# Half-pair transposes in two PSUM banks, joined decay sums and paired mixer tiles in a chunked recurrence with a token mixer

## The chip, the cores and the metric

The kernel runs on one core of a Trainium2 chip. Five engines work side by side and meet at semaphores: TensorE (PE in the profile; PEld is its weight load), VectorE (DVE), ScalarE (ACT), GpSimd (POOL) and SyncE (SP), which only issues DMA here. PE writes only into PSUM, eight banks of 2 KB on each of 128 partitions; DVE and ACT read PSUM, POOL does not. The metric is the time of one execution on the device in microseconds (us).

## The reference

Two stages, in float32 outside and bfloat16 in the matmuls. The first is a linear recurrence per batch and head (4 batches, 8 heads, 768 tokens, 40 features):

```python
for t in range(S):
    y[:, :, t] = np.einsum('bhd,bhde->bhe', rt, state)
    Sa = np.einsum('bhde,bhe->bhd', state, at)
    state_decay = state * wt[:, :, None, :] - np.einsum('bhd,bhe->bhde', Sa, bt)
    state = state_decay + np.einsum('bhd,bhe->bhde', vt, kt)
```

The second takes the heads side by side as x (4 x 768 x 320) and mixes tokens, then channels:

```python
theta = x @ w_theta
zr, zi = x * np.cos(theta), x * np.sin(theta)
yr = np.einsum('ts,bsd->btd', w_tok_r, zr)
yi = np.einsum('ts,bsd->btd', w_tok_i, zi)
u = x + yr + yi
return (u + np.maximum(u @ w_ch, 0.0)).astype(np.float32)
```

## The kernel before

**Tiles.** A tile is 128 tokens of one batch, all 8 heads: 6 tiles a batch, 24 in all. The recurrence is done a tile at a time, with the state carried between the tiles of a batch.

**Attention of one tile.** `prep` (L439) takes the logarithm of w, sums it down the tokens by a matmul with a triangle (L461), and gets the decay products by Exp (L469). A second set, without the token's own decay, is needed for a and for the output: for the first 7 tiles (`EXCLUSIVE`) by another triangle matmul (L476) and Exp (L479), later by DVE adding the logarithm back (L482) and an Exp (L487). k and b are multiplied by the one set and a by the other (L429), and all are cast to bfloat16. Then kb, a and v are transposed on PE, 128 x 128 blocks against an identity (L391), into one bank a tensor, and copied out by ACT or DVE (L394, L397). For the first 8 tiles (`RUNS`) v, and for all tiles r, come by DMA in runs of eight tokens and are transposed by `turn_runs` (L538); `turn_back` (L557) makes the token-major v of the first 8. Eleven groups, listed in `CROSSBAR`, are transposed by DMA on SP's queue instead (L698).

`attention_scores` and `readout` form four 128 x 128 score blocks per head (psi, phi, lamv, lamu) with matmuls of 64 rows, two heads at once on the two halves of the array into two banks (L569). Each result is masked by DVE while it leaves PSUM (L578), or scaled by ACT (L580) and then masked by POOL's select (L582). `recurrence` solves for the tile (x0 L610 and L616, nx, nu L629) and makes the new state gt (L652). From the fifth tile on (`FROM_POOL`) DVE adds the old state (L663) and POOL multiplies by the decay (L667); before that PE adds it by an identity matmul (L647). `readout` forms y (L793, L800, L802), and L809 scales it to x.

**Mixer.** `theta` transposes two tiles of x as five blocks (L711) and multiplies them by w_theta: two matmuls a tile over 128 rows (L763) and, for the 64 rows that are left of each, one of half height, the two side by side (L773). Results are copied tile by tile (L828). When a batch's tiles are through, `sines` takes Sin in two groups of three tiles (L850), which needs another table of ACT, and POOL multiplies (L865), zr and zi apart. `mix_row` sums 12 matmuls for each output tile (L881), `channels` multiplies by w_ch in the same way as theta, and each output tile is stored by its own DMA (L920). The rows of one batch run between the attention of the next.

**Order.** The order of all work is written out: `add` collects the operations, and `Plan.order` emits them by the list `ORDER`. `PICK` names those that run on their second engine, `HOMES` gives each PSUM result its bank, from four single banks and two pairs, and `WARM` puts 49 idle matmuls before some early operations. Each engine runs its own operations in this order.

Of the kernel before, what the change touches and what calls it, by code (L numbers as in the profile page):

```python
# [17 lines left out]
BANKS = 8  # L18
DOUBLE = 4
FROM_POOL = 4  # L20
EXCLUSIVE = 7
RUNS = 8
LAST = (22, 23)
CROSSBAR = (("tkb", 23), ("ta", 23), ("tv", 22), ("tv", 23), ("xt", 18), ("xt", 20), ("ut", 12), ("ut", 14),
            ("ut", 16), ("nut", 21), ("nut", 22))
ORDER = [
# [118 lines left out]
WARM = {21: 25, 30: 4, 33: 1, 28: 8, 41: 11}  # L145


class Op:
# [908 lines left out]
```

## Time and profile before

| | |
|---|---|
| two runs | 199.07 and 200.09 us, median 199.58 |
| profiled execution, first to last instruction | 197.8 us |
| granted TensorE clock | 1.00 |
| HBM read, written | 29.54 MB, 3.93 MB |
| input load, issue to landing (raw_w, raw_r) | 4.1, 4.4 us |

Most lines of the profile give an engine, an operation, output<-inputs by the program's names, shapes and a count, then busy time in us and mean length in ns, and behind a second bar the idle time of the engine just before, with what ended it. `128*128` in front of the shapes is the part of the array that is used; `64*128` is half its rows. In the answers by stage, each stretch has the busy time and the count of instructions of PE, PEld, DVE, ACT and POOL, then the granted clock, the share of the DMA engines and GB/s.

### The profile page before, as it was taken

The page shows a single profiled execution, that of the slowest core. Times are in us where ns is not written, and L with a number is a line of the kernel's source. Part 1 is how long each engine was busy: PE and PEld are TensorE (multiplying, and loading weights), DVE is VectorE, ACT ScalarE, POOL GpSimd, SP SyncE. Part 2 cuts the span into 40 slices and gives each one's busy share as a digit, 9 for nine tenths or more (in the row PEclk, how much of TensorE's full clock was granted, in tenths as well). Part 3 has the DMA queues.
Part 4 walks back from the last instruction along what each step waited for, and adds up shares of the span by engine and source line. Part 5 has one row for each costly group of instructions (what it writes and reads, how often), then busy time and mean ns, then how long its engine had stood idle before and what let it go on. Part 6 is the DMA issues. An engine that isn't in the chain of part 4 may idle for free.

```text
span 197.8 us, 8019 instructions
## 1 busy us (share of the span) xinstructions
PE 187.6 (95%) x3288; PEld 150.3 (76%) x3288; DVE 164.3 (83%) x261; ACT 151.7 (77%) x337; POOL 145.1 (73%) x210
## 2 busy tenths in 40 slices
PE   7888999999989999999999999999999999999992
PEld 6776787777768788878878888888887878767661
DVE  5269899999989999888887988999999988675453
ACT  3584979799889988979988598888998986575111
POOL 8267544679879999699799939769699697558100
PEclk9999999999999999999999999999999999999999
DMA  6999879989999999999998899988998274863055
GB/s 119 210 212 163 154 161 196 182 166 197 233 174 173 207 171 185 190 185 223 153 210 168 153 187 170 188 148 169 182 155 163 43 177 102 87 194 104 0 191 174
DMA packets 134644, 32.75 MB, mean 166 GB/s; under 512 B 124816, under 2 KB 134608, under 8 KB 134608
## 3 DMA queue, kind: packets, MB, share of 16 engines
q1 hardware_dynamic: 131680, 29.19, 75.1%
q0 software_dynamic: 2784, 2.97, 9.6%
q8 instruction: 25, 0.41, 0.9%
q10 hardware_dynamic: 144, 0.08, 0.1%
q14 instruction: 11, 0.09, 0.1%
HBM read 29.54 MB, written 3.93 MB: 169 GB/s over the span
## 4 chain that ended last, share of the span: by engine, by line
PE 68%; DMA 9%; ACT 8%; SPq 6%; DVE 3%; issue 3%; POOL 1%; ACTq 0%; DVEq 0%; POOLq 0%
PE ps_s L881 17%; PE ps_s L391 10%; PE ps_d L569 9%; PE ps_s L763 5%; SPq L409 4%; DMA raw_w<-in_w_dram 3%; DMA raw_kb<-in_k_dram 3%; PE ps_s L711 3%; PE ps_s L652 2%; PE ps_s L629 2%; SPq L421 2%; DMA raw_r<-in_r_dram 2%; PE ps_s L538 2%; PE ps_s L773 2%; ACT cs L850 2%
## 5 line engine op out<-in xcount | busy, mean ns | idle before, releaser
L429 POOL TENSOR_TENSOR kb<-raw_kb,ex 128x320 bf16<-128x320 f32 x46 | 36.8, 811 | 9.7 <-DMA raw_kb<-in_k_dram 3.3
L881 PE MATMUL ps_s<-zr,wtok_r 128*128 128x320 bf16 x132 | 37.6, 299 | 0.0
L881 PE MATMUL ps_s<-zi,wtok_i 128*128 128x320 bf16 x132 | 37.5, 299 | 0.0
L578 DVE TENSOR_TENSOR lamu<-ps_d,mask_p 128x1024 bf16<-128x1024 f32 x22 | 26.8, 1219 | 1.7 <-PE ps_d L569 1.6
L578 DVE TENSOR_TENSOR psi<-ps_d,mask_p 128x1024 bf16<-128x1024 f32 x22 | 26.8, 1218 | 1.6 <-PE ps_d L569 1.4
L578 DVE TENSOR_TENSOR lamv<-ps_d,mask_p 128x1024 bf16<-128x1024 f32 x17 | 20.7, 1218 | 2.6 <-PE ps_d L569 1.8
L429 POOL TENSOR_TENSOR ah<-raw_a,we 128x320 bf16<-128x320 f32 x22 | 19.0, 866 | 3.6 <-DMA raw_a<-in_a_dram 1.6
L578 DVE TENSOR_TENSOR phi<-ps_d,mask_n 128x1024 bf16<-128x1024 f32 x17 | 20.7, 1218 | 0.9 <-PE ps_d L569 0.8
L865 POOL TENSOR_TENSOR zi<-cs,xp 128x320 bf16<-128x320 f32 x21 | 16.9, 816 | 3.3 <-ACT cs L850 3.3
L881 PEld LDWEIGHTS <-wtok_r 128*128 128x128 bf16 x144 | 14.0, 97 | 4.5
L569 PE MATMUL ps_d<-aT,kbT 64*128 64x128 bf16 x384 | 17.1, 217 | 0.2
L881 PEld LDWEIGHTS <-wtok_i 128*128 128x128 bf16 x144 | 14.1, 98 | 3.5
L391 PE MATMUL ps_s<-wide,kb 128*128 128x128 bf16 x184 | 15.0, 223 | 1.0 <-POOL kb L429 0.7
L865 POOL TENSOR_TENSOR zr<-cs,xp 128x320 bf16<-128x320 f32 x19 | 15.3, 810 | 0.7 <-ACT cs L850 0.7
L667 POOL TENSOR_TENSOR gt<-sum,ex 128x320 bf16<-128x320 f32 x13 | 9.5, 733 | 8.0 <-DVE sum L663 4.8
L800 PE MATMUL ps_s<-kb,lamv 128*128 128x40 bf16 x192 | 15.0, 180 | 0.0
L802 PE MATMUL ps_s<-kb,lamu 128*128 128x40 bf16 x192 | 14.9, 179 | 0.0
L569 PEld LDWEIGHTS <-kbT 64*128 64x128 bf16 x384 | 11.8, 94 | 3.1 <-ACT kbT L394 1.0
L800 PEld LDWEIGHTS <-lamv 128*128 128x128 bf16 x192 | 13.2, 96 | 0.6
L887 DVE TENSOR_TENSOR up<-ps_s,xp 128x320 bf16<-128x320 f32 x22 | 10.7, 488 | 3.5 <-PE ps_s L881 3.1
L435 POOL CAST r<-raw_r 128x640 bf16<-128x640 f32 x12 | 8.6, 720 | 6.5 <-DMA raw_r<-in_r_dram 6.5
L445 ACT ACTIVATE lw<-raw_w 128x320 bf16<-128x320 f32 x24 | 11.4, 475 | 2.6 <-DMA raw_w<-in_w_dram 2.6
(176 smaller groups left out, 606.7 us busy)
## 6 DMA issues: line engine op xcount, KB each, us to landing
raw_w<-in_w_dram SPq DMA_DIRECT2D x24, 160.0 KB, 4.1
raw_v<-in_v_dram SPq DMA_DIRECT2D x24, 160.0 KB, 3.9
raw_a<-in_a_dram SPq DMA_DIRECT2D x24, 160.0 KB, 4.2
raw_kb<-in_k_dram SPq DMA_DIRECT2D x24, 160.0 KB, 3.7
raw_kb<-in_b_dram SPq DMA_DIRECT2D x24, 160.0 KB, 4.0
raw_r<-in_r_dram SPq DMA_DIRECT2D x24, 160.0 KB, 4.4
out_dram<-oo SPq DMA_DIRECT2D x9, 160.0 KB, 2.0
wrow_i<-in_moe_w_tok_i_dram POOLq DMA_DIRECT2D x6, 192.0 KB, 5.3
```

The source lines that it names most:

```text
L391: nc.tensor.transpose(out=dst[:, c:c + 128], in_=pair(src, g), identity=ident)
L429: pool = ("POOL", lambda: nc.gpsimd.tensor_tensor(out=dst, in0=in0, in1=in1, op=ALU.mult))
L445: add("ACT", "ln", i, lambda: nc.scalar.activation(out=paired(lw)[:, :, :, 0:D], in_=paired(raw_w[s4]), func=AF.Ln), 473, [("raw_w", s4)], ...
L569: nc.tensor.matmul(t[:, q, g, :], lhsT=lhs[g][rows(q)], rhs=rhs[g][rows(q)], start=True, stop=True)
L578: add("DVE", kindm, i, lambda: nc.vector.tensor_tensor(out=flat, in0=whole(), in1=mask.to_broadcast([128, 2 * G, 128]), op=ALU.mult), 1217 ...
L667: add("POOL", "wgt", i, lambda: nc.gpsimd.tensor_tensor(out=new_state, in0=sum_t, in1=wm.to_broadcast([128, 8, D]), op=ALU.mult), 830, [(" ...
L763: nc.tensor.matmul(ps(pk)[:, 0:DM], lhsT=lhs[:, 3 * c + kt, :], rhs=wt[:, 3 * c + kt, :], start=kt == 0, stop=kt == 2, skip_group_check=n ...
L800: nc.tensor.matmul(o, lhsT=lamv[:, p, g, :], rhs=kb[:, 0, h, 0:D], start=first, stop=False, skip_group_check=True)
L802: nc.tensor.matmul(o, lhsT=lamu[:, p, g, :], rhs=kb[:, 1, h, 0:D], start=False, stop=True, skip_group_check=True)
L865: pool = ("POOL", lambda: nc.gpsimd.tensor_tensor(out=dst, in0=in0, in1=in1, op=ALU.mult))
L881: nc.tensor.matmul(acc(), lhsT=wtok[nm][j][:, s], rhs=zs[c][:, s], start=n == 0 and c == 0, stop=n == NT - 1 and c == 1)
L887: add("DVE", "uadd", q, lambda: nc.vector.tensor_tensor(out=u, in0=acc(), in1=x, op=ALU.add), 488, [pk, x_key(q)], [u_key(q)], at="row")
```

## The change

- **Transposes.** `half_turns` transposes a 128-row block as two halves of 64 rows, one on each half of the array, each into its own bank of a pair. k, b and a of a tile go as one group of 12 blocks with one copy (`kbaT`), r and v of two tiles as one group (`turned`); after the eighth tile v has a group of its own for two tiles. Small groups (nu, x, u, `turn_back`) go either way, by `PICK`. DMA transposes are gone.
- **Decay.** The second decay sum is always a matmul with the strict triangle, into the bank beside the first, and one Exp reads both (`decays`). The DVE step L482 and the second Exp are gone. From the third tile on, k and b are one product of twice the width.
- **State.** The old state is always added by the identity matmul in `gt_mm`, and DVE alone makes the new state.
- **Mixer.** theta and channels run for two tiles as six matmuls over 128 rows into two banks, with zero rows in the weights in place of the half-height matmuls. One copy or one output step serves both tiles, one DMA stores both, and zr and zi are one product. Sin takes two groups of three tiles, and for the last batch four, one and one.
- **Order.** `ORDER`, `PICK`, `HOMES` and `WARM` are new. Any operation may use any bank, 96 idle matmuls are placed, and which engine copies, masks and multiplies is chosen anew for every operation.

The core of the diff:

```diff
-FROM_POOL = 4
-EXCLUSIVE = 7
+SPLIT = 2
...
+    def half_turns(key, srcs, first=0):
+        if plan.home[key][1] == 1:
+            for n, src in enumerate(srcs):
+                nc.tensor.transpose(out=block(bf(ps(key)), first + n), in_=src, identity=ident)
+            return
+        for n, src in enumerate(srcs):
+            for c in range(2):
+                to = bf(ps(key)[:, c])[:, (first + n) * 64:(first + n) * 64 + 64]
+                nc.tensor.transpose(out=to, in_=src[rows(c)], identity=ident[rows(c), rows(c)])
...
+            nc.tensor.matmul(sums(1)[:, :, 0:D], lhsT=mask_p[:, 0, :], rhs=lw[:, :, 0:D],
+                             start=True, stop=not total_of(i), skip_group_check=True)
+            if total_of(i):
+                nc.tensor.matmul(sums(1)[:, :, D], lhsT=mask_p[:, 0, :], rhs=lw[:, :, 63],
+                                 start=False, stop=True, skip_group_check=True)
...
+                nc.scalar.activation(out=ex.rearrange("p c h x -> p c (h x)"),
+                                     in_=ps(pk)[:, :, 0:DM + 8], func=AF.Exp)
...
+            product("kb", i, kb[:, :, :, 0:D], raw_kb[i % NK],
+                    ex[:, 0:1, :, 0:D].to_broadcast([128, 2, H, D]),
...
+        add("PE", "tkba", i, lambda: half_turns(
+            key, [pair(s, g) for s in (kb[:, 0], kb[:, 1], ah) for g in range(G)]),
...
-                add("POOL", "wgt", i, lambda: nc.gpsimd.tensor_tensor(
-                    out=new_state, in0=sum_t, in1=wm.to_broadcast([128, 8, D]), op=ALU.mult), 830,
...
-        def both():
-            for c in range(2):
-                nc.tensor.matmul(ps(("ps", kind, q + c))[:, 0:DM], lhsT=lhs[rows(c), 2, :],
-                                 rhs=wt[rows(c), 2, :], start=False, stop=True,
-                                 skip_group_check=True)
+        def both():
+            for c in range(2):
+                for kt in range(3):
+                    nc.tensor.matmul(ps(key)[:, c, 0:DM], lhsT=block(lhs, 2 * c + kt),
+                                     rhs=wt[:, 3 * c + kt, :], start=kt == 0, stop=kt == 2)
...
+            product("z", q, z[:, :, j], cs_t[:, :, j],
+                    x.rearrange("p (o d) -> p o d", o=1).to_broadcast([128, 2, DM]),
...
+WARM = {62: ((0, 42),), 114: ((1, 17),), 40: ((2, 20),), 28: ((4, 17),)}
```

More of the change, by code (lines that the diff above doesn't have):

```diff
@@ new lines, in gt_mm @@
+        def gt_mm():
+            t = ps(gk)
+            if not first:
+                nc.tensor.matmul(t[:, 0:DM], lhsT=ident,
+                                 rhs=gt_old.rearrange("p g c d -> p (g c) d")[:, :, 0:D],
+                                 start=True, stop=False, skip_group_check=True)
+            for g in range(G):
+                for j, (lt, rt) in enumerate(((kb[:, 0], vb), (kb[:, 1], nu))):
+                    nc.tensor.matmul(t[:, g * 80:g * 80 + 80], lhsT=pair(lt, g),
+                                     rhs=rt[:, 2 * g:2 * g + 2, 0:D],
+                                     start=first and j == 0, stop=j == 1, skip_group_check=True)
@@ L887, in mix_row, with chunk @@
+        x, u, z = x_of(q), u_of(q), z_t[bi % 2]
+        for s in range(NT):
+            def chunk(s=s):
+                for c in range(2):
+                    nc.tensor.matmul(ps(pk)[:, 0:DM], lhsT=wtok[j][:, c, s], rhs=z[:, c, s],
+                                     start=s == 0 and c == 0, stop=s == NT - 1 and c == 1)
+            add("PE", "row", q, chunk,
+                [("z", 0, bi % 2, s), ("z", 1, bi % 2, s), ("wtok", j)], [pk],
+                new=(pk, 1) if s == 0 else None)
         add("DVE", "uadd", q, lambda: nc.vector.tensor_tensor(
-            out=u, in0=acc(), in1=x, op=ALU.add), 488,
@@ new lines, in channels @@
+        ends = q == N - 1
+        halves = [slice(0, DM // 2), slice(DM // 2, DM)] if ends else [slice(0, DM)]
+        mixed("ch", q, uT_t[n], wch, [("wch", c) for c in range(6)], ("uT", n), halves)
+        bi, j = divmod(q, NCH)
+        place = (q + 1) // 2 % NO
+        oo = oo_t[place]
+        if not alone(q):
+            ck = ("ps", "ch", q)
+            add("DVE", "oo2", q, lambda: nc.vector.scalar_tensor_tensor(
+                out=oo.rearrange("p (c d) -> p c d", c=2), in0=ps(ck)[:, :, 0:DM], scalar=0.0,
+                in1=src.rearrange("p (c d) -> p c d", c=2), op0=ALU.max, op1=ALU.add),
+                [ck] + [u_key(t) for t in group], [("oo", place)])
+            store(q, out_p[bi, j // 2], oo.rearrange("p (c d) -> p c d", c=2), ("oo", place))
+            return
@@ new lines, in channels @@
+        for part, at in enumerate(halves):
+            ck = ("ps", "ch", q + part)
+            key = ("oo", place) if part == 0 else ("last", 1)
+            add("DVE", "oo1" if not ends else "ooh", q + part, lambda ck=ck, at=at:
+                nc.vector.scalar_tensor_tensor(
+                    out=oo[:, at], in0=ps(ck)[:, 0:at.stop - at.start], scalar=0.0,
+                    in1=u_of(q)[:, at], op0=ALU.max, op1=ALU.add),
+                [ck, u_key(q)] + ([("oo", place)] if part else []), [key])
+            store(q + part, out_r[bi, j, :, at], oo[:, at], key,
+                  nc.scalar if ends and part == 0 else nc.sync)
@@ L984 @@
+    for i in range(4):
         loads(i)
+    turned(0)
     prep(0)
     attention_scores(0)
-    loads(3)
     mixer_weights()
```

844 lines of the change are left out of this document (346 added, 498 removed), and 224 rows, old and new, of tables (HOMES, ORDER, PICK).

## The prediction

> **What bounds the kernel now.** I read the page's busy times and slices first, then the busy time by stage.
>
> ```profile
> span 197.8 us, 8019 instructions
> ...
> PE 187.6 (95%) x3288; PEld 150.3 (76%) x3288; DVE 164.3 (83%) x261; ACT 151.7 (77%) x337; POOL 145.1 (73%) x210
> ...
> PE   7888999999989999999999999999999999999992
> ```
>
> ```profile
> 0.00:20.00 20.00, 16.66 (x235) 13.76 (x235) 12.43 (x41) 11.39 (x25) 12.55 (x35) 1.00 0.92 176
> 20.00:60.00 40.00, 37.46 (x758) 30.38 (x758) 37.00 (x46) 34.91 (x88) 28.18 (x38) 1.00 0.95 183
> 60.00:150.00 90.00, 89.46 (x1690) 73.68 (x1689) 81.57 (x119) 79.38 (x176) 78.79 (x109) 1.00 0.99 179
> 150.00:190.00 40.00, 40.00 (x581) 30.14 (x578) 29.62 (x51) 25.06 (x48) 25.57 (x31) 1.00 0.51 113
> ```
>
> The columns are PE, weight loads, DVE, ACT, POOL, granted clock, DMA share, GB/s. From 60 to 190 us PE is busy 129.46 of 130 us: the token-mixing rows (L881) of one batch fill every gap that the attention of the next leaves. Before 60 us hardly a row is ready; there DVE (37.00 of 40) is as full as PE, and most of these waits on loads lie there:
>
> ```profile
> POOL r L435 <- DMA raw_r<-in_r_dram: 6.5, 5, 2.5
> POOL kb L429 <- DMA raw_kb<-in_k_dram: 3.3, 3, 1.7
> ```
>
> The clock is granted in full, so a change pays by taking work from PE after 60 us, or by bringing the first rows forward. The sum is made against the 197.8 us of the profiled execution; the runs have 199.58 in the median, so 1.8 us lie outside the span.
>
> **PE's prices.** Matmuls overlap, so the cost of one is the spacing of starts, not its length. The timeline (start, length, engine) gives it.
>
> ```profile
> 104.38 0.20 PE L652 MATMUL ps_s<-v,kb 128*128 128x80 bf16 x1
> 104.42 0.20 PE L652 MATMUL ps_s<-nu,kb 128*128 128x80 bf16 x1
> 104.55 0.40 PE L569 MATMUL ps_d<-rT,vT 64*128 64x128 bf16 x8
> 104.80 0.39 PE L569 MATMUL ps_d<-rT,nuT 64*128 64x128 bf16 x8
> 105.12 0.19 PE L800 MATMUL ps_s<-kb,lamv 128*128 128x40 bf16 x1
> ...
> 105.33 0.18 PE L800 MATMUL ps_s<-kb,lamv 128*128 128x40 bf16 x1
> 105.36 0.18 PE L802 MATMUL ps_s<-kb,lamu 128*128 128x40 bf16 x1
> 105.38 0.18 PE L800 MATMUL ps_s<-kb,lamv 128*128 128x40 bf16 x1
> ```
>
> ```profile
> 145.05 0.39 PE L391 MATMUL ps_s<-wide,v 128*128 128x128 bf16 x4
> 145.27 0.39 PE L391 MATMUL ps_s<-wide,nu 128*128 128x128 bf16 x4
> 145.50 0.30 PE L881 MATMUL ps_s<-zr,wtok_r 128*128 128x320 bf16 x1
> 145.63 0.30 PE L881 MATMUL ps_s<-zi,wtok_i 128*128 128x320 bf16 x1
> 145.77 0.30 PE L881 MATMUL ps_s<-zr,wtok_r 128*128 128x320 bf16 x1
> 145.91 0.30 PE L881 MATMUL ps_s<-zi,wtok_i 128*128 128x320 bf16 x1
> ```
>
> ```profile
> L569 PE MATMUL ps_d<-aT,kbT 64*128 64x128 bf16 x384 | 17.1, 217 | 0.2
> ...
> L773 PE MATMUL ps_s<-wth,xT 64*128 64x320 bf16 x22 | 3.4, 307 | 0.0
> ```
>
> A whole 128-column transpose takes 56 ns (eight from 145.05 to 145.50), a 320-column matmul 136 (145.50 to 145.91, three), a 40-column one 25; so 0.417 ns a column and 2.5 beside, never under 25. In half-height mode two matmuls on the two row halves run together: the 22 of L773, eleven pairs, are busy 3.4 us in all, 0.31 us a pair, the 307 ns of one alone. Eight of L569 (four pairs) last 0.40 us with 0.217 for the last, so a pair of 128 columns takes (0.40 - 0.22) / 3 = 60 ns, 4 more than one matmul. A change of mode costs some 92 ns: 104.42 to 104.55 is 130 ns where 36 would do, and the last pair of 104.80 starts at 104.97, 150 before 105.12 where 60 would do.
>
> **The change on PE, part by part** (counts from the two programs' instruction lists).
>
> Transposes: before, 749 whole ones at 56 ns, 41.9 us. After, 143 whole (8.0 us) and 659 half pairs of 64 columns; the 53 more are the eleven groups that DMA transposed. No row shows such a pair. From below it takes 64 x 0.417 = 27 ns, from above as much as a whole transpose, 56. I take 64 x 0.417 + 2.5 + the 4 of pairing = 33, since L569 is the same mode and pairing with twice the columns: 21.7 us. Together 29.7, so -12.2; by the bounds -16.1 to +3.0.
>
> Decay sums: the second is now always a matmul, 17 more of 320 columns (2.3 us) and 20 of 8 (0.5): +2.8. State: 13 more tiles add the old state by an identity matmul, 13 x 136 ns: +1.8. Mixer weights: two tiles took 4 x 136 ns and one half-height pair of 136 + 4, now 6 x 136 with zeroed halves: +132 ns, 22 times, +2.9. Mode changes fall from 134 to 122: -1.1. The 47 more warm-up matmuls (2.6 us) lie in waits of the first 20 us, covered by the loads; without that cover they cost their 2.6.
>
> Sum: -12.2 + 2.8 + 1.8 + 2.9 - 1.1 = -5.8 us of PE.
>
> **Where that lies.** At these prices the two programs add up, warm-ups included, to 176.6 and 173.3 us. Up to the readout of the seventh tile (at 61 us before) they hold 47.0 and 46.0, the second with 2.4 us of rows already and 2.7 more of warm-ups. So 129.6 remain before and 127.3 after: 2.3 us count for sure if the rest stays as dense. The other saving lies in the first 60 us and pays only as far as that stage shortens. DVE's work up to that tile falls by 1.3 us (49.5 to 48.2, counts times spacing), and from the fifth tile on the state no longer goes over DVE and then POOL (L667 below, 0.73 us a tile), of which I count 1 us for the tiles before 60. 2.3 + 1.3 + 1.0 = 4.6 us.
>
> **The other engines.**
>
> ```profile
> L578 DVE TENSOR_TENSOR psi<-ps_d,mask_p 128x1024 bf16<-128x1024 f32 x22 | 26.8, 1218 | 1.6 <-PE ps_d L569 1.4
> L482 DVE TENSOR_TENSOR sx<-ps_s,lw 128x320 f32<-128x320 f32 x17 | 8.2, 487 | 2.7 <-ACT ex L469 2.4
> L580 ACT ACTIVATE lamv<-ps_d 128x1024 bf16<-128x1024 f32 x7 | 7.2, 1028 | 2.4 <-PE ps_d L569 2.2
> L469 ACT ACTIVATE ex<-ps_s 128x328 f32<-128x328 f32 x20 | 9.0, 449 | 2.0 <-PE ps_s L464 1.4 <-POOL gt L667 0.3
> L850 ACT ACT_TABLE_LOAD x5 | 6.4, 1283 | 0.1
> L667 POOL TENSOR_TENSOR gt<-sum,ex 128x320 bf16<-128x320 f32 x13 | 9.5, 733 | 8.0 <-DVE sum L663 4.8 <-PE ps_d L569 3.2
> L582 POOL TENSOR_SCALAR_AFFINE_SELECT phi<-phi 128x1024 bf16<-128x1024 bf16 x7 | 7.6, 1093 | 1.0 <-ACT phi L580 1.0
> L429 POOL TENSOR_TENSOR kb<-raw_kb,ex 128x320 bf16<-128x320 f32 x46 | 36.8, 811 | 9.7 <-DMA raw_kb<-in_k_dram 3.3 <-ACT ex L469 2.8 <-ACT aT L394 1.6
> ```
>
> DVE: 20 masks fewer (20 x 1.218 = -24.4) and no sx (-8.2); in their place 32 copies and negations out of PSUM from ACT, eight of them double (+17.8 at 487 ns a single and, between 487 and 1218, some 820 a double), some 6 us of evacuations and 10 of products. The sum stays within 2 us. ACT: 20 masks more (20 x 1.028 = +20.6) and four table loads (+5.1); one Exp of 656 lies between 449 (328 columns) and 1028 (1024), some 0.72 against two of 0.45, so -5; copies and evacuations handed over or joined, -16: about +5, beside 10.6 us of its idle time from 60 to 150. POOL: 20 selects more (+21.9), no gt (-9.5), and 32 double products for pairs of single ones and seven ah to DVE; no row has a double one, between 0.81 and 1.62, I take 1.5, near two: -26, about -13 in all. SP issues eleven stores and eleven transposes fewer. The cover of all this is PE's own work; if it went, ACT's 5 us would show first.
>
> **Rivals.**
>
> *The first stage opens up* (0.22). PE was idle 3.3 us before 20 and 2.5 from 20 to 60. If the larger groups and the shorter state chain bring the rows forward, all 5.8 us and 5 of the idle go: 197.8 - 10.8 + 1.8 = 189. For it: 18 row matmuls now stand before the seventh tile's readout, none before. Against it: the loads' bytes are the same.
>
> *A half pair costs two instructions* (0.13). The 25 ns of L800 and L802 are then paid by each half: 659 x (50 - 33) = +11.2, PE's sum becomes +5.4, time 205. It decides from 42 ns a pair. For it: the shortest matmuls shown stay 25 ns apart; against it: the pairs of L773 and L569. The Trainium skill ("TensorE: Matmul & The Clock Gate", "Wait — 56ns, not 53.3ns?") says that starts never come closer than about 25 ns, however short the matmul. Taken for every instruction that gives these 50 ns, and the term for transposes would be -0.9 us; the 0.31 us a pair in L773 disagrees across row halves, and no run here shows it for so few columns.
>
> *Two-bank groups leave PE waiting* (0.12). One group of 24 halves now waits for three products and two free banks, and its copy of 768 words, by the same two ACT rows, holds them some 0.8 us; what stands behind it in PE's queue waits too, scores and rows. With PE idle 8% of its last 127 us, 10 us come: 199.6 - 4.6 + 10 = 205. From 3.6% on the gain is gone. For it: ACT and DVE are 88 and 91% full from 60 to 150; against it: they were so with PE at 99%.
>
> *DVE and POOL in each other's way* (0.13).
>
> ```profile
> L865 POOL TENSOR_TENSOR zr<-cs,xp x19: 782/790/1052, 51.7 to 181.1; 128x320 bf16<-128x320 f32 x19
> ...
> L864 DVE TENSOR_TENSOR zr<-cs,xp x3: 623/969/1077, 159.8 to 179.1; 128x320 bf16<-128x320 f32 x3
> ```
>
> A product of two SBUF tiles on DVE takes 623 to 1077 ns beside such products on POOL, where 487 is its usual length. DVE had 10 of them, now 24 worth 37 single ones: 27 x 0.5 = 13 us more if all overlap. DVE has 8.4 us idle from 60 to 150 and 3 from 20 to 60, so some 2 to 5 us pass through, and the gain is gone: 200. None overlapping costs nothing.
>
> *My forecast* (0.40): 197.8 - 4.6 + 1.8 = 195.0, with its own range from 193.5 (all of the 5.8) to 197.5 (2.3 alone).
>
> **The numbers.** A measurement can tell 2% from no change, so faster is under 195.6 and slower over 203.6. Faster: 0.24 of the forecast and all of the first rival, 0.46. Slower: the half pairs' 0.13, 0.10 of the waiting banks, 0.02 of the engines in each other's way, 0.25. The rest is 0.29: 0.16 of the forecast, 0.11 and 0.02. The range goes from 187, with the first rival's 189 in it, to 206, which takes in both at 205.
>
> **What would show it.** Right: a group of 24 halves (twelve pairs) in 0.4 us of starts and not 0.6; PE's busy share above 98% from 60 to 190; the seventh tile's readout before 60 us; DVE's sum unchanged. Wrong: halves starting 25 ns apart; PE idle behind banks or kb after 60 us; DVE products near 1 us; or a first stage that ends well under 58 us.

## The result, and the profile after

The changed kernel takes 208.69 us (median of 2 runs, 208.41 and 208.98) where the kernel before takes 199.58: 1.0434 times as long, with an interval of 1.0318 to 1.0551. It is slower; the forecast was 195.0 us, and the range ended at 206. The profiled execution has a span of 206.7 us against 197.8. Here and in the table of the experiments the ratios are those of the fast runs, while the times are medians of all runs.

From the page of the changed kernel: the busy times, the slices of PE and of the granted clock, and the groups of the joined operations.

```profile
span 206.7 us, 9451 instructions
...
PE 185.8 (90%) x4097; PEld 148.7 (72%) x4097; DVE 170.7 (83%) x260; ACT 153.8 (74%) x243; POOL 139.3 (67%) x161
...
PE   7886599987988999999799799999898999979992
...
PEclk9999889999999999999999999999999999999998
...
L429 POOL TENSOR_TENSOR z<-cs,xp 128x640 bf16<-128x640 f32 x14 | 22.6, 1623 | 10.1 <-ACT cs L776 10.1
...
L473 ACT ACTIVATE ex<-banks 128x656 f32<-128x656 f32 x20 | 14.4, 720 | 3.2 <-PE banks L467 2.9
...
L374 ACT COPY kbaT<-banks 128x768 f32<-128x768 f32 x15 | 12.1, 805 | 0.4 <-PE banks L357 0.3
```

The busy times by stage, with the columns of the prediction's table:

```profile
0.00:20.00 20.00, 15.49 (x313) 13.57 (x315) 10.47 (x35) 9.68 (x15) 14.07 (x37) 1.00 0.91 172
20.00:60.00 40.00, 34.13 (x951) 28.66 (x945) 35.42 (x50) 34.58 (x58) 30.01 (x34) 0.96 1.06 198
60.00:150.00 90.00, 86.00 (x1970) 67.98 (x1969) 82.41 (x115) 76.92 (x119) 69.58 (x69) 1.00 0.95 177
150.00:190.00 40.00, 37.48 (x778) 29.27 (x776) 34.35 (x47) 29.23 (x45) 24.22 (x21) 1.00 0.24 62
```

From 60 to 190 us PE is now busy 123.5 of 130 us, where it was busy 129.5. No other engine has become full: DVE has 116.8 of these 130 us, against 111.2 before. PE waits again and again, for a little.

Matmuls overlap, so busy time hides part of that. A sharper count takes the distance between the starts of neighbouring matmuls in the trace: up to the price of the first (the prediction's prices, a change of mode included, two halves counted as one pair) it is work, what lies above is a gap. So counted, PE's work falls from 175.4 to 170.9 us (-4.5), and its gaps rise from 17.5 to 30.9 (+13.4); the sum is the +8.9 of the span. Each gap of over 20 ns I put to what ended last among the things that the next operation needs, by the lists of the two programs and the ends in the traces:

| gaps, us | before, to 60 us | after, to 60 us | before, from 60 | after, from 60 |
|---|---|---|---|---|
| a bank was not yet read out by its earlier user | 2.0 | 3.9 | 1.9 | 5.2 |
| data of POOL came last | 3.2 | 3.7 | 0.04 | 2.4 |
| data of DVE came last | 0.6 | 0.7 | 0.1 | 2.2 |
| data of ACT came last | 3.0 | 3.7 | 0.8 | 1.5 |
| waits ahead of idle matmuls, and no one late | 3.7 | 5.5 | 0 | 0 |
| all | 12.4 | 17.6 | 2.9 | 11.3 |

The waits of PE and POOL in the profile of the changed kernel (who waits <- for whom: us in total, times, the longest) name the same places:

```profile
PE banks L357 <- DVE lamu L574: 1.8, 2, 1.1
PE banks L518 <- POOL r L435: 1.7, 1, 1.7
...
PE banks L799 <- POOL z L429: 1.0, 2, 0.6
PE banks L799 <- DVE z L428: 1.0, 1, 1.0
PE banks L352 <- ACT gd L389: 1.0, 1, 1.0
PE banks L357 <- POOL kb L429: 0.9, 2, 0.6
...
POOL z L429 <- ACT cs L776: 13.5, 6, 4.5
POOL lamv L578 <- ACT lamv L576: 11.0, 5, 4.2
```

The first row is a wait for a bank: the group of kb and a (L357) waits until DVE has read lamu out of the bank that it is to use. The third and the fourth are data: the token rows (L799) wait for z. And POOL, which is only 67% busy, stands 13.5 us waiting for sines and 11.0 for ACT's lamv before it does what PE then waits for.

Two suspects come out of this. DVE's products of two SBUF tiles have become long, and so have POOL's beside them:

```profile
L428 DVE TENSOR_TENSOR z<-cs,xp 128x640 bf16<-128x640 f32 x8 | 10.4, 1298 | 1.7 <-ACT cs L776 1.7
...
L428 DVE TENSOR_TENSOR kb<-raw_kb,ex 128x640 bf16<-128x640 f32 x5 | 6.4, 1283 | 0.0
L428 DVE TENSOR_TENSOR ah<-raw_a,ex 128x320 bf16<-128x320 f32 x7 | 6.3, 893 | 0.2 <-DMA raw_a<-in_a_dram 0.2
```

Alone, a double one takes 0.83 us (the shortest of the eight z) and a single one 0.48. Each of the 24 taken against the shortest of its shape, the excess is 9.1 of their 25.0 us, against 1.6 for the ten before; in the same way all of POOL's operations exceed their shortest by 10.5 us, where it was 4.1. The other suspect is the new plan as a whole: larger groups in banks, a new order, other engines.

### The profile page after: what moved, and what is told of

Read it like the earlier page. It is cut to its first block, busy times and chain, and to the rows that moved or that the text cites. A ratio compares the mean times of both kernels' runs of the same rounds, so it can differ in the third digit from the quotient of the medians.

```text
span 206.7 us, 9451 instructions
## 1 busy us (share of the span) xinstructions
PE 185.8 (90%) x4097; PEld 148.7 (72%) x4097; DVE 170.7 (83%) x260; ACT 153.8 (74%) x243; POOL 139.3 (67%) x161
## 4 chain that ended last, share of the span: by engine, by line
PE 52%; DVE 13%; ACT 11%; SPq 10%; DMA 5%; issue 4%; POOL 2%; DVEq 0%; ACTq 0%; POOLq 0%
PE banks L799 11%; SPq L400 10%; PE banks L566 8%; PE banks L709 7%; PE banks L357 6%; ACT cs L776 4%; PE banks L352 3%; DMA raw_kb<-in_b_dram 3%; DVE lamu L574 3%; DVE z L428 3%; PE banks L645 2%; DMA raw_r<-in_r_dram 2%; ACT L776 2%; PE banks L621 2%; PE banks L736 1%
## 5 line engine op out<-in xcount | busy, mean ns | idle before, releaser
L799 PE MATMUL banks<-z,wtok 128*128 128x320 bf16 x288 | 49.3, 299 | 2.0 <-POOL z L429 1.0
L799 PEld LDWEIGHTS <-wtok 128*128 128x128 bf16 x288 | 24.5, 97 | 10.7 <-issue 2.4
L429 POOL TENSOR_TENSOR kb<-raw_kb,ex 128x640 bf16<-128x640 f32 (+1 forms) x19 | 27.0, 1424 | 6.2 <-DMA raw_v<-in_v_dram 2.4
L429 POOL TENSOR_TENSOR z<-cs,xp 128x640 bf16<-128x640 f32 x14 | 22.6, 1623 | 10.1 <-ACT cs L776 10.1
L578 POOL TENSOR_SCALAR_AFFINE_SELECT lamv<-lamv 128x1024 bf16<-128x1024 bf16 x17 | 19.8, 1163 | 11.2 <-ACT lamv L576 11.0
L574 DVE TENSOR_TENSOR lamu<-banks,mask_p 128x1024 bf16<-128x1024 f32 x20 | 24.4, 1219 | 3.4 <-PE banks L566 3.0
L574 DVE TENSOR_TENSOR psi<-banks,mask_p 128x1024 bf16<-128x1024 f32 x15 | 18.3, 1220 | 3.4 <-PE banks L566 3.4
L574 DVE TENSOR_TENSOR phi<-banks,mask_n 128x1024 bf16<-128x1024 f32 x16 | 19.5, 1217 | 0.3 <-PE banks L566 0.2
L576 ACT ACTIVATE lamv<-banks 128x1024 bf16<-128x1024 f32 x17 | 17.5, 1030 | 2.9 <-PE banks L566 2.6
L566 PE MATMUL banks<-kbaT 64*128 64x128 bf16 x384 | 18.1, 217 | 0.4 <-ACT ex L473 0.2
L578 POOL TENSOR_SCALAR_AFFINE_SELECT psi<-psi 128x1024 bf16<-128x1024 bf16 x9 | 10.4, 1157 | 7.2 <-ACT psi L576 5.9
L734 PEld LDWEIGHTS <-lamv 128*128 128x128 bf16 x192 | 13.4, 97 | 1.0 <-issue 0.4
L357 PE MATMUL banks<-wide,kb 64*128 64x64 bf16 x384 | 10.0, 190 | 3.0 <-DVE lamu L574 1.1
L374 ACT COPY kbaT<-banks 128x768 f32<-128x768 f32 x15 | 12.1, 805 | 0.4 <-PE banks L357 0.3
```

The lines of the kernel that those rows point to most:

```text
L357: nc.tensor.transpose(out=to, in_=src[rows(c)], identity=ident[rows(c), rows(c)])
L429: pool = ("POOL", lambda: nc.gpsimd.tensor_tensor(out=dst, in0=in0, in1=in1, op=ALU.mult))
L566: nc.tensor.matmul(t[:, q, g, :], lhsT=lhs()[g][rows(q)], rhs=rhs()[g][rows(q)], start=True, stop=True)
L574: add("DVE", "m" + kind, i, lambda: nc.vector.tensor_tensor(out=flat, in0=whole(), in1=mask.to_broadcast([128, 2 * G, 128]), op=ALU.mult), ...
L576: [key], [dkey], alts=(("ACT", lambda: nc.scalar.mul(out=flat, in_=whole(), mul=sign)),))
L578: ("POOL", lambda: nc.gpsimd.affine_select(out=flat, in_=flat, pattern=[[0, 2 * G], [1, 128]], compare_op=ALU.is_gt, fill=0.0, base=0, cha ...
```

## The experiments

Four questions, one after the other: is it the division of the work between engines, is it PE's own price, can another order repair it, and which single load carries the cost. The table holds the medians (us), that of the kernel before on the same chip, and the ratio with its interval.

| kernel | time | before | ratio |
|---|---|---|---|
| the change itself | 208.69 | 199.58 | 1.0434 (1.0318 to 1.0551) |
| p_products_to_pool | 236.46 | 200.47 | 1.1863 (1.1729 to 1.1998) |
| m_masks_to_dve | 258.37 | 200.47 | 1.2811 (1.2576 to 1.3046) |
| pmc_engines_as_before | 270.77 | 200.47 | 1.3571 (1.3454 to 1.3688) |
| w_whole_transposes | 219.07 | 200.47 | 1.0980 (1.0884 to 1.1076) |
| order_replanned | 233.02 | 200.51 | 1.1544 (1.1412 to 1.1676) |
| order_for_products_on_pool | 230.43 | 200.51 | 1.1499 (1.1389 to 1.1609) |
| order_for_engines_as_before | 233.82 | 200.51 | 1.1606 (1.1481 to 1.1730) |
| order_and_engines_free | 234.56 | 200.51 | 231.26 to 237.92 us, no ratio on record |
| same_engines_new_order | 214.27 | 199.16 | 1.0748 (1.0680 to 1.0815) |
| products_on_pool_new_order | 214.92 | 199.16 | 1.0767 (1.0693 to 1.0840) |
| engines_as_before_new_order | 219.33 | 199.16 | 1.1017 (1.0951 to 1.1083) |
| free_engines_new_order | 218.58 | 199.16 | 1.0990 (1.0919 to 1.1060) |
| c_products | 205.30 | 200.65 | 1.0242 (1.0172 to 1.0311) |
| c_masks | 208.51 | 200.65 | 1.0380 (1.0292 to 1.0469) |
| d_after | 208.67 | 200.65 | 1.0405 (1.0326 to 1.0485) |
| d_before | 198.36 | 200.65 | 0.9900 (0.9867 to 0.9934) |
| c_selects | 207.32 | 199.47 | 1.0403 (1.0354 to 1.0451) |
| e_clock | 210.21 | 199.47 | 1.0546 (1.0489 to 1.0602) |

The kernel before itself moves by 1.5 us through this table (199.16 to 200.65), so about 1 us between rows with different values of it says little.

### Other engines in the same order

Order and banks stay as in the change; operations are given back to the engine that had them before, 18 products to POOL in the first, the masks in the second (29 go to DVE and 9 to ACT and POOL, 20 more on DVE in all), and both with the copies in the third. The edits are entries of `PICK` alone, here the first two of the 18:

```diff
-    160: 1, 210: 1
```

> The changed kernel with 18 of its 24 DVE products of two SBUF tiles (kb of tiles 4, 8, 15, 20, 21; ah of 3, 5, 8, 11, 13, 19; z of 4, 5, 9, 11, 12, 15, 19) given back to POOL; order, banks and everything else stay. If DVE and POOL in each other's way is what cost the time (DVE's products are 9.1 us longer than alone, POOL's operations 10.9), most of it goes: 200 to 203 us, with DVE's double products gone and POOL's double products back at 1.42 us. If the masks made by ACT and POOL together are the cause, POOL gets some 20 us more to do while it still waits 21 us for ACT's masks: 209 to 214. If the first stage alone is the cause, within 1 us of the changed kernel's 208.7.

> The changed kernel with its masks divided as before the change (18 by ACT and POOL, 70 by DVE, the same tiles as before; the changed kernel has 38 and 50 of the 88). DVE gets 20 x 1.22 = 24 us more, ACT loses 21, POOL 22. If the masks that go over ACT and POOL one after the other make PE wait (POOL waits 21 us for ACT's masks), 203 to 206 in spite of a DVE that is then about full (170.7 + 24 = 195 us busy). If DVE is what counts, 212 to 218. If products of DVE and POOL in each other's way are the cause, the overlap stays and DVE gets fuller: 212 or more.

> The changed kernel with products, masks and the small copies out of PSUM (nx, the negated nu, gd, theta) on the engines that had them before the change; half pairs, groups, banks, the joint Exp, order and loads stay as changed. Busy by counts: DVE about 155 us, ACT 149, POOL 145, as before the change. If the new division of work over the engines is the cause, by whichever of the two ways, the forecast's gain comes back: 195 to 199. If the order (first tile's output 8 us later, mixer weights fetched earlier) or the two-bank groups are the cause, 204 to 209. Between these, both.

They took 236, 258 and 271 us. In the first, PE's waits (same columns as above) show the reason:

```profile
PE banks L973 <- POOL z L603: 12.5, 6, 3.9
PE banks L531 <- POOL kb L603: 7.1, 5, 2.9
```

A product that is put into POOL's queue at the place that was meant for DVE's stands behind selects whose input comes later, and the rows and transposes stand behind it in PE's queue. And where PE waits for long, its clock goes too, down to the 5 in this row of the third kernel's slices, with 0.888 in the mean:

```profile
PEclk9998899985899987979559779999979999569998
```

So these three say nothing of the cause. They say that the order was made for this division: to change the division alone costs some 28 us or more.

### PE's own price: whole transposes

The half pairs become one whole transpose each, into the same two banks read as one row, with the copies to match; 531 of the 659 pairs (the rest are those of `turn_runs`).

```diff
+        flat = bf(ps(key)).rearrange("p c w -> p (c w)")
         for n, src in enumerate(srcs):
-            for c in range(2):
-                to = bf(ps(key)[:, c])[:, (first + n) * 64:(first + n) * 64 + 64]
-                nc.tensor.transpose(out=to, in_=src[rows(c)], identity=ident[rows(c), rows(c)])
+            nc.tensor.transpose(out=block(flat, first + n), in_=src, identity=ident)
```

> The changed kernel with the 531 half pairs of the groups of kb and ah, v, the mixer's weights and the two-bank groups of nu, x and u as whole transposes into the same two banks, copied out as one row; only the 128 pairs of r and v by tokens stay halves. If a pair costs the 35 ns that the trace shows against 56, PE's work grows by 531 x 21 ns = 11 us, less some mode changes: 213 to 219. If PE's idle time (31 us) swallows it, 209 to 211, and PE's price is then not what counts in the changed kernel. If half pairs cost more than they look, by holding weight loads or banks, below 206.

It took 219.07 us, 10.4 more than the change. The groups of kb and a by line and shape, first of the change, then of this kernel:

```profile
L357 PE MATMUL banks<-wide,kb 64*128 64x64 bf16 x384 | 10.0, 190 | 3.0 <-DVE lamu L574 1.1 <-POOL kb L429 0.9 <-ACT phi L576 0.6
L357 PE MATMUL banks<-wide,ah 64*128 64x64 bf16 x192 | 6.9, 190 | 0.0
```

```profile
L356 PE MATMUL banks<-wide,kb 128*128 128x128 bf16 x192 | 14.9, 219 | 1.9 <-DVE lamu L571 0.9 <-ACT phi L573 0.6 <-POOL kb L426 0.4
L356 PE MATMUL banks<-wide,ah 128*128 128x128 bf16 x96 | 9.3, 219 | 0.0
```

16.9 us of busy time against 24.2, with twice the instructions. By starts PE's work goes from 170.9 to 185.2, the gaps only from 30.9 to 27.2. Half pairs earn some 10 us; the change is slower in spite of them. The two-bank groups are the same here, and the gaps stay.

### New orders

Can the loss be planned away? Eight kernels keep the changed kernel's operations and get an order, banks and idle matmuls of my own, found by a list scheduler (`ORDER`, `HOMES`, `WARM`; the engines too where the name says so). The first four took a load to land sooner than it does. The edit, in its first entries, is of this kind (here same_engines_new_order):

```diff
-ORDER = [8, 0, 32, 61, 62, 1, 2, 33,
+ORDER = [50, 0, 32, 8, 33, 34, 2, 36,
...
-WARM = {62: ((0, 42),), 114: ((1, 17),), 40: ((2, 20),), 28: ((4, 17),)}
+WARM = {28: ((7, 17),), 40: ((7, 20),), 62: ((7, 42),), 114: ((7, 17),)}
```

> The first four runs moved work between engines under an order that had been made for another division, so they could not tell the division from the order. Here and in the next three the order of all operations and the banks are made anew by one and the same list scheduler, which has the durations of this case's traces; the 96 warm-up matmuls become 42. This kernel keeps the changed kernel's division over the engines. If the changed kernel's order is poor in itself, it gets faster by 3 us or more, 203 to 206. If that order is as good as its division allows (the cause is the division or the shared SBUF side of DVE and POOL), 207 to 212.

> The same with the 18 DVE products of two SBUF tiles on POOL, and an order made for that. If products of DVE and POOL in each other's way cost the time (20 us more busy time in the two together), this is 4 us or more faster than the replanned kernel that keeps them: 198 to 203. If they cost nothing in the end, within 2 us of it. If POOL, with 22 us more of its own, becomes the bound, 4 us or more slower.

> The same with masks, products and small copies on the engines that had them before the change, and an order made for that. It took 270.8 us under the changed kernel's order. If the division is the cause, 195 to 200, faster than the replanned kernel with the new division by 5 us or more. If it is the order alone, both come within 3 us of each other. If the new division suits the groups and the joint Exp better than the old one, slower than that kernel by 2 us or more.

> Order, banks and engines chosen anew together, for the same operations (43 of the 88 masks by ACT and POOL, 22 products on DVE, 181 of 452 choices other than in the changed kernel; the division in numbers hardly moves). If order and choices, which go together, are what the changed kernel got wrong, and its half pairs, groups and joint Exp are sound, 191 to 197, the forecast's 195 with it. If two-bank groups, the joined work or DVE and POOL in each other's way limit it whatever the order, 203 or more.

They took 230 to 235 us, whatever the division: starved of loads early on (in order_replanned POOL waits 12.1 us for raw_r, 6.5 before the change), with long stretches at half clock (0.92 in the mean). The next four start from the changed kernel's order, with loads as slow as the traces show and the clock in the plan:

> The scheduler of the four replanned kernels took loads to land faster than they did (a 160 KB load of w, k, b or a held the queue some 1.05 us on the chip) and knew nothing of the granted clock, which fell to half after a stretch with PE idle; its orders let loads come late, at 0.92 to 0.93 of the clock. Here it has both, and starts from the changed kernel's own order, moving single operations. Division over the engines, operations and warm-up matmuls are the changed kernel's; order and banks are new. If the changed kernel's order, loads included, is what cost the time, 198 to 203 us. If the division, the shared SBUF side of DVE and POOL, or the groups are the cause, no order helps: 206 to 210.

> As the kernel before in this call, but with the 18 DVE products of two SBUF tiles on POOL. If DVE and POOL in each other's way cost time that no order takes back, 3 us or more faster than that kernel. If the order decides and the overlap is absorbed in idle time, within 2 us of it.

> As the first kernel of this call, but masks, products and small copies on the engines that had them before the change (18 masks by ACT and POOL, not 38). 270.8 us under the changed kernel's order. If the new division, with POOL waiting for ACT's masks, is the cause, 3 us or more faster than the first kernel of this call. If only the fit of order and division counts, within 3 us of it, 198 to 206.

> As the first kernel of this call, with engines chosen along with the order. If the changed operations are sound, this is the best of the four, 196 to 201, at or under the kernel before. If two-bank groups or the joined work stand in the way, no better than the first one, and over 203.

All four expectations of a gain were missed: 214 to 219 us. The 18 products on POOL gave 214.92 against 214.27 with them on DVE, the outcome named for an overlap that is absorbed; the old division gave 219.33, 5 us more. Read by starts, the four tell two things besides.

| us | PE's work | changes of mode | first matmul | gaps |
|---|---|---|---|---|
| before | 175.4 | 134 | 1.1 | 17.5 |
| the change | 170.9 | 122 | 1.1 | 30.9 |
| same_engines_new_order | 178.0 | 194 | 4.3 | 27.9 |
| products_on_pool_new_order | 177.8 | 192 | 5.1 | 29.3 |
| engines_as_before_new_order | 179.1 | 208 | 5.1 | 29.3 |
| free_engines_new_order | 178.6 | 212 | 4.0 | 32.5 |

First, my orders lost by a price that the changed kernel's order avoids: in the first of the four 72 more changes of mode at the prediction's 92 ns are 6.6 of the 7.1 us of added work, and PE begins 3 us later. Second, the gaps are 28 to 32 us with every division between engines, DVE's products or POOL's, the old masks or the new. So under these orders the old division doesn't remove them; how much of each sum is the order's own, the runs don't tell.

### One load left out at a time

Here order, banks, queues and waits stay those of the change, and one kind of work is cut short.

> The changed kernel, its order and engines untouched, with 16 of DVE's products of two SBUF tiles (19.1 us in the profile) cut to an eighth of their columns: kb of tiles 4, 8, 15, 20, 21, ah of 3, 5, 8, 11, 13, 19, z of 9, 12, 15, 19, 21; the rest of those tiles keeps old values. It takes some 17 us from DVE and the overlap from POOL. If DVE and POOL in each other's way is the main price, 201 to 204. If only DVE's load counts, as much as the next kernel gains. If neither, 207 to 209.

```diff
+        def few(t):
+            if (kind, i) not in CUT:
+                return t
+            n = t.shape[-1] // 8
+            return t[:, :, 0:n] if len(t.shape) == 3 else t[:, :, :, 0:n]
-        dve = ("DVE", lambda: nc.vector.tensor_tensor(out=dst, in0=in0, in1=in1, op=ALU.mult))
+        dve = ("DVE", lambda: nc.vector.tensor_tensor(out=few(dst), in0=few(in0), in1=few(in1), op=ALU.mult))
```

> The control for the kernel before: the masks of lamu on DVE for 18 tiles cut from eight blocks to one (18 x 1.0 = 18 us less on DVE, nothing from the overlap with POOL); the other seven blocks keep old values. If DVE's load is what counts, the same gain as with the products, 201 to 205. If the overlap counts, half of that gain or less: 206 to 209.

```diff
+        n = 1 if kind == "lu" and i in CUT else 8
-            out=flat, in0=whole(), in1=mask.to_broadcast([128, 2 * G, 128]), op=ALU.mult),
+            out=flat[:, 0:n], in0=whole()[:, 0:n], in1=mask.to_broadcast([128, n, 128]), op=ALU.mult),
```

The pages' busy times, of the kernel with short products and of that with short masks:

```profile
PE 184.5 (91%) x4097; PEld 147.9 (73%) x4097; DVE 161.6 (80%) x260; ACT 153.3 (76%) x243; POOL 132.6 (65%) x161
```

```profile
PE 185.0 (90%) x4097; PEld 148.3 (72%) x4097; DVE 156.1 (76%) x260; ACT 153.5 (75%) x243; POOL 138.9 (68%) x161
```

Short masks (18 of lamu) take 14.6 us off DVE and give 0.2 us of time by the medians; by the ratios 1.1 us, with intervals that overlap. Short products (16 of the 24) take 9.1 off DVE, and POOL, whose work is unchanged, gets 6.7 us shorter, nearly the whole growth of its excess; that gives 3.4 us (205.30 against 208.69; 3.2 and 3.4 against the 208.51 and 208.67 of the two kernels beside it on the same chip). The time lies between the ranges expected for the main price and for none: these products are one price among several. It isn't how full DVE is that counts, but where these products stand: on data that PE waits for, and against POOL. How much of the 3.4 is their own length and how much the engines' stopping each other, the run doesn't separate. The stage from 60 to 190 us of the kernel with short products shows where it comes back:

```profile
60.00:190.00 130.00, 126.72 (x2783) 99.98 (x2776) 110.84 (x164) 108.28 (x169) 89.92 (x92) 1.00 0.75 143
```

126.7 us of PE against 123.5. That the first 60 us don't move (gaps of 18.9 us against 18.3, by starts) leaves their loss to something else.

The loads come next, k, b and a cut to half their bytes from tile 5 on, in the changed kernel and in the one before:

```diff
+        few = H // 2 if i >= 5 else H
-        load("la", i, raw_a[i % NA], src_of(a, i), ("raw_a", i % NA))
+        load("la", i, raw_a[i % NA][:, 0:few], src_of(a, i)[:, 0:few], ("raw_a", i % NA))
```

> The changed kernel with half as many bytes in the loads of k, b and a from tile 5 on (four of the eight heads; the other heads keep older values). If loads that land late for this order hold the changed kernel up, 202 to 205. If not, within 2 us of 208.7.

> The kernel before the change with the same lighter loads. If late loads are the changed kernel's price alone, this stays within 1.5 us of the kernel before (PE was 99.6% busy from 60 to 190 us). If both kernels wait for loads alike, it gains as much as the changed kernel does, and loads explain nothing of the difference.

208.67 us: nothing. The kernel before gains 1% (198.36 against 200.65), a little more than was expected. Behind the first five tiles, whose loads stay whole, the changed kernel isn't slower because it waits for k, b and a; the loads of w, r, v and the weights weren't cut.

Then POOL's selects, the other long work in its queue, and the stretch at half clock in the first stage:

```diff
-                out=flat, in_=flat, pattern=[[0, 2 * G], [1, 128]], compare_op=ALU.is_gt,
+                out=flat[:, 0:1], in_=flat[:, 0:1], pattern=[[0, 1], [1, 128]], compare_op=ALU.is_gt,
```

> The changed kernel with POOL's 38 selects cut from eight blocks to one (38 x 0.95 = 36 us less on POOL and on the way of those masks) and ACT's scale set to zero, so that these 38 masks leave out their scores; ACT's time, the order and the engines are unchanged. If the two-step masks are a price of their own, 203 to 206. If the products beside POOL are all that POOL costs, the selects among what they overlap with, 205.5 to 207.5. If neither, 207.5 to 209.

```diff
-WARM = {62: ((0, 42),), 114: ((1, 17),), 40: ((2, 20),), 28: ((4, 17),)}
+WARM = {62: ((0, 42),), 114: ((1, 17),), 40: ((2, 20),), 28: ((4, 17),), 107: ((7, 28),)}
```

> The changed kernel with 28 more warm-up matmuls (1.6 us at full clock) where PE waits for the cast of r at 21.7 us. If the wait is what takes the clock away, it stays at 1.00 from 20 to 28 us. If the half clock is what the first stage lost, the first outputs come 1 to 2 us earlier and the end 1 to 2 us too, 206.5 to 207.7. If waits for loads and engines take that back, within 0.5 us of the changed kernel's 208.7, with the clock full all the same.

Short selects, which take 31.6 us off POOL (139.3 to 107.7), give 1.4 us of time by the medians and 0.6 by the ratios; the ratio's interval lies within that of the change, so no gain is shown. The 28 idle matmuls keep the clock, and the time gets longer by 1.5 us (2.2 by the ratios). The stretches before, in and after the half clock (columns as above, the granted clock third from the end), of the change:

```profile
20.79:24.20 3.41, 1.68 (x62) 1.25 (x58) 2.29 (x4) 1.96 (x3) 2.89 (x4) 1.00 1.10 211
24.20:27.61 3.41, 2.88 (x46) 2.54 (x43) 3.19 (x4) 1.71 (x3) 2.67 (x3) 0.50 0.84 203
27.61:31.03 3.42, 3.06 (x92) 2.49 (x91) 2.54 (x4) 3.27 (x6) 0.10 (x1) 1.00 1.06 215
```

and of the kernel with the idle matmuls:

```profile
20.79:24.20 3.41, 3.04 (x79) 2.58 (x77) 2.24 (x4) 1.90 (x3) 2.50 (x4) 1.00 1.08 209
24.20:27.61 3.41, 2.72 (x71) 2.17 (x64) 2.63 (x3) 2.10 (x5) 3.02 (x3) 1.00 0.73 184
```

The clock is 1.00 where it was 0.50, and nothing is won. The idle matmuls fill the wait as meant: the transposes of r behind them start at 23.76 us where they started at 23.45. Yet the seventh tile's readout comes at 69.5 us where it was 67.2; why, this run doesn't show. Of that expectation the half on the clock held, and the half on the time didn't.

## Why the prediction was wrong, point by point

**The step that failed** is "2.3 us count for sure if the rest stays as dense". It did not stay dense. Behind 60 us PE's gaps went from 2.9 to 11.3 us, and that is 8.4 us against a saving of 4.5. The second step that failed is the 1.3 and 1.0 us that it added for the first 60 us: there the gaps grew by 5.2 us, and no rival let that stage become slower, which takes the time beyond the range's 206. The prediction had itself put the point where the gain is gone at 3.6% of idle PE; by busy time PE is idle 5.0% from 60 to 190. It said that "the cover of all this is PE's own work". That cover is what the change thinned out: with less work and larger pieces on PE, whatever comes late shows. And it wasn't "ACT's 5 us" that showed first: from 60 us on, the gaps behind banks grew by 3.3 us, behind POOL by 2.4, behind DVE by 2.1 and behind ACT by 0.7.

**PE's prices were right.** The work fell by 4.5 us by starts, where the two programs' prices (176.6 and 173.3) gave 3.3. The timeline has the group of 24 halves as forecast:

```profile
130.02 0.41 PE L566 MATMUL banks<-rvT,nuT 64*128 64x128 bf16 x8
130.27 0.39 PE L357 MATMUL banks<-wide,kb 64*128 64x64 bf16 x16
130.50 0.28 PE L357 MATMUL banks<-wide,ah 64*128 64x64 bf16 x8
130.71 0.45 PE L799 MATMUL banks<-z,wtok 128*128 128x320 bf16 x2
```

Eight pairs from 130.27 to 130.50 are 29 ns a pair; the whole group ends within 0.44 us, the change of mode included, where 33 ns and 92 were reckoned. The rival that each half pays 25 ns is out, and the kernel with whole transposes shows the term's worth: 10.4 us.

**The first stage did not shorten.** The multiplication by the state's readout (x, L742 after) first runs at 27.5 us where it was 19.1, and for the seventh tile at 67.2 where it was 62.0 (the first of before, then the first and the seventh after):

```profile
19.14 0.48 DVE L809 TENSOR_TENSOR xp<-ps_s,we 128x320 bf16<-128x320 f32 x1
...
27.54 0.47 DVE L742 TENSOR_TENSOR xp<-banks,ex 128x320 bf16<-128x320 f32 x1
...
67.19 0.48 DVE L742 TENSOR_TENSOR xp<-banks,ex 128x320 bf16<-128x320 f32 x1
```

So the 1.3 and 1.0 us that DVE and the state chain should have brought forward didn't come, nor did the first rival (0.22). PE's gaps there grew by 5.2 us, and none of the cuts moved them (18.3 us in the change with the gaps under 20 ns; 18.9, 18.1, 18.6, 18.6 and 17.3 with short products, masks, loads, selects and with the clock kept). The largest single wait is 1.7 us for POOL's cast of r (L518). One term of the prediction bears on it: the 47 more idle matmuls, put at nothing because the loads would cover them, and at 2.6 us without that cover. By starts and the prediction's prices, both kernels have some 7.4 us of gaps up to 20 us, but the changed one has spent 5.5 us of work on idle matmuls where it was 2.7, and has done 6.2 us of other matmuls where it was 8.9. Whether they stood in the way or filled waits that the new order has, no run shows, as none left them out. Why this stage is slower is open; the loads of its first five tiles weren't cut in any run either.

**DVE and POOL in each other's way** (0.13) is real in the rows. The 3.4 us with 16 of the 24 products cut short lie within its "2 to 5 us", but the cut takes the products' own length too, so they are no measure of the overlap alone. The rival by itself ends at 200, not at 208.7. The two engines in the timeline of the change (start, length, engine; DVE's, then POOL's):

```profile
183.74 0.83 DVE L428 TENSOR_TENSOR z<-cs,xp 128x640 bf16<-128x640 f32 x1 [1.27 <-ACT cs L776]
...
185.83 2.03 DVE L428 TENSOR_TENSOR z<-cs,xp 128x640 bf16<-128x640 f32 x1
...
183.79 3.39 POOL L429 TENSOR_TENSOR z<-cs,xp 128x640 bf16<-128x640 f32 x2 [4.49 <-ACT cs L776]
187.13 1.68 POOL L578 TENSOR_SCALAR_AFFINE_SELECT lamv<-lamv 128x1024 bf16<-128x1024 bf16 x1
```

The first DVE product begins 0.05 us before POOL's pair and takes its usual 0.83; the second begins while POOL is at work and takes 2.03. POOL's two take 3.39 instead of twice 1.42.

**Two-bank groups leave PE waiting** (0.12) is what the gaps point to for the rest: waits for a bank grew by 3.3 us from 60 us on and by 1.9 before, and gaps of some 27 us or more stayed in every kernel that kept these groups, 27.2 with whole transposes in them, where the kernel before has 17.5. That is an argument from the traces. No run took the groups apart with all else equal, so this cause isn't shown.

**Sums of the engines.** "The sum stays within 2 us" for DVE missed: +6.4, and the products' excess alone grew by 7.5. The rest of that working holds: without the excess DVE is 1.1 us lower. POOL fell by 5.8 and not 13, for the same reason (6.4 us more of excess). ACT rose by 2.1 and not 5. The single prices were right: 0.72 us for the Exp of 656, 0.80 for a copy of 768 words, 1.42 for a double product undisturbed (1.5 was taken). Two sums of the prediction are off by little: all of the 5.8 us gives 193.8 and not 193.5, and 50 ns a pair gives -1.0 for the transposes and not -0.9.

**The account.** Of the 8.9 us of span: PE's work -4.5; gaps +13.4, of which DVE's products 3.4 (shown, their own length and the overlap with POOL together), the first stage 5.2 (open), and the rest, some 5, for waits for banks and longer chains (argued), with perhaps 1 for POOL's selects in it.

No kernel here that does the whole work is faster than the kernel before.

## What to carry to other kernels

Where one engine is full because it fills every gap from a stock of waiting work, a saving on it counts only as far as the others can deliver sooner; price the others' lateness first, not their busy sums. Joining small operations saves instructions, but the join waits for its last input and holds its banks until its one copy is done; what that cost here is argued, not shown. An order written out for one division of work can be a poor one for another (236 to 271 us here): after any change of engine, plan again, and count changes of mode in the plan.

## What the runs showed of the hardware

**The clock gate looks at fixed windows.** The granted clock changes only on a grid of 3.41 us. In the change it is halved behind a window in which PE was busy 1.68 of 3.41 us. One of the reordered kernels (order_and_engines_free) shows more of it, in the stretches on its own grid:

```profile
12.33:15.74 3.41, 2.26 (x43) 1.40 (x42) 1.50 (x3) 2.04 (x2) 2.25 (x4) 0.50 1.15 188
15.74:19.15 3.41, 2.45 (x36) 1.60 (x34) 1.02 (x4) 1.50 (x4) 2.19 (x3) 0.50 0.83 139
19.15:22.56 3.41, 3.22 (x64) 2.78 (x64) 2.30 (x3) 2.77 (x5) 3.41 (x5) 0.50 1.07 182
22.56:25.97 3.41, 3.11 (x103) 2.69 (x103) 2.13 (x4) 3.41 (x6) 3.41 (x5) 1.00 1.14 229
25.97:29.38 3.41, 2.18 (x61) 1.59 (x55) 2.68 (x5) 1.46 (x3) 1.73 (x3) 1.00 1.21 217
29.38:32.79 3.41, 0.51 (x18) 0.51 (x20) 0.16 (x1) 1.09 (x2) 2.28 (x4) 0.50 0.78 132
```

A window with 2.18 us of work is followed by half clock; windows with 2.26 and 2.45 us don't bring it back, one with 3.22 does, and in the change one with 2.88 did. Busy time alone isn't the rule: in order_replanned the window from 36.55 us, at full clock with 2.04 us of PE, is followed by full clock, and in order_for_products_on_pool the one from 22.52 us, at half clock with 3.23 us, by half. The Trainium skill ("TensorE: Matmul & The Clock Gate", "What's actually happening") gives a free-running window of 3413 ns, which the trace agrees with, and says that the clock drops after at least one idle window; here a window that was only half idle was enough.

**A stopped product waits, it doesn't work more slowly.** With short products, from the timeline:

```profile
112.56 0.24 DVE L437 TENSOR_TENSOR z<-cs,xp 128x80 bf16<-128x80 f32 x1 [0.23 <-ACT cs L785]
...
114.66 0.84 DVE L437 TENSOR_TENSOR kb<-raw_kb,ex 128x80 bf16<-128x80 f32 x1
...
114.02 1.39 POOL L438 TENSOR_TENSOR ah<-raw_a,ex 128x320 bf16<-128x320 f32 x1
```

An eighth of a double product takes 0.24 us or 0.84, the latter ending 0.09 us after POOL's product that was under way. Of the 16 short products nine took 0.45 to 1.44 us, and each of these ended 0.06 to 0.10 us after an operation of POOL; the other seven took 0.24 us or less. The Trainium skill ("SBUF — State Buffer", "Who interferes with whom") says that a DVE instruction with two SBUF inputs contends with a GpSimd instruction that reads SBUF, that the contention is an exclusive lock, and that a DVE instruction with at most one SBUF input doesn't contend; these rows agree, and so does DVE's mask of lamu out of PSUM, which has one SBUF input and took 1219 ns in the mean in the change as before.

**The 25 ns between matmuls hold for a pair, not for each half.** In the groups of 64-column halves a pair mostly takes 28 to 30 ns. In 338 of the 603 pairs that another follows, the halves start mostly 3 to 4 ns apart and the next pair 25 to 26 ns behind that; in most of the others the halves start 16 to 20 ns apart, and the next pair 9 to 12 behind. The Trainium skill ("TensorE: Matmul & The Clock Gate", "Measured speedup vs the span model") counts about 4 ns of issue for each further tile of the array that works beside the first, and the trace agrees for these 338; the floor of its other section, on which the prediction's second rival leaned, isn't paid by each half.
